# A fused attention and two-layer expert kernel: the last 768 tokens of the feed-forward in three parts of 256, with first-layer results in idle output banks

## The chip, the cores and the metric

The kernel runs on one core of one Trainium2 chip. The metric is device time in microseconds (us) for one execution, as the median of three runs. TensorE (PE in the profile), VectorE (DVE), ScalarE (ACT), GpSimd (POOL) and SyncE (SP, which issues most transfers) run side by side, each in the order of its own instructions. PE's clock has two levels, 2.4 and 1.2 GHz; the profile shows the granted one as 1.00 and 0.50.

## The reference, cut to what matters

```python
attn = softmax(mean_pool(q) @ k.T / 8) @ v            # 4 x 8 heads, 576 queries, 1152 keys
x = attn.reshape(2304, 512)                           # tokens
h = x @ w_in                                          # 512 -> 2048
x = (h * cos(h)) @ w_out                              # 2048 -> 512
e = argmax(x @ w_gate)                                # one of 8 experts per token
out = gate[:, None] * (relu(x @ w1[e]) @ w2[e])       # 512 -> 1024 -> 512, rows of one expert together
```

## The kernel before

The program has three stages: attention, feed-forward, experts. In the second and third each float32 product is three products of numbers cut into a high and a low part (high x high, high x low, low x high), so there are three matmuls where one would do.

**Feed-forward.** The 2304 tokens come in four chunks of 512 and one of 256 (`xT[d]`, 512 = `DC`, 256 = `CH`). For each chunk, `high(d)` and `low(d)` make the two parts of the tokens (`xh` by ACT, `xl` by DVE), and then sixteen steps f = 0..15 go over the 2048 hidden columns, 128 at a time. Step f is

- `layer1(d, f)` (L900): 12 matmuls of 512 (or 256) columns into one PSUM bank `h`;
- the function h cos h on ACT and DVE: a (L907, ACT), L908 to L910 (DVE), r (L911, ACT), a again (L912, ACT), L913 (DVE, the last reader of `h`: after it the bank is free), then the high part g (L914, ACT) and the low part g (L915, DVE);
- `layer2(d, f)` (L924): three matmuls for each 128 tokens into the output banks `po`, which gather over all sixteen f. It is issued two steps behind `layer1` (`LAG`, the list `todo`), three in the last chunk.

PSUM has eight banks: `ps_h` 2 (for `h`), `ps_o` 4 (one `po` for each 128 tokens), `ps_m` 2 (everything small). A chunk of 512 fills all four of `ps_o`, the last chunk two. With two banks, `layer1` of step f+2 needs L913 of step f.

When a chunk is done, `rows` copies the `po` out (L812) and one `epilogue` for each 256 tokens computes which expert each token goes to (transposes L820, products L828 to L838, counting in the class `Router`). The epilogues are generators; `go_on` takes two steps of them after each f, three in the last chunk. The epilogue of the last tokens but 256 also finds the expert of the first slot (`first`, PE line L581, then a short chain on DVE to the expert's number) and has its 4 MB of weights loaded (`load(0)`: eight transfers of 512 KB on SP, L709 and L711). From step 9 of the last chunk on, `conv(0, j)` cuts these weights into high and low part, one transfer at a time (w: ACT L718, then DVE L719).

**Experts.** Sixteen slots, in turn 256 and 128 rows of one expert. `gather`, `split` (transposes L738, then the two parts of the tokens xe: ACT L689, DVE L690), `compute` (L764 or L781 into `ph`, relu, L802 into `po`), result scattered to DRAM. Weights and tokens of slot i+1 are made ready during slot i. The xe of one slot fill all four tiles of the pool `xlp`.

The attention stage has its order from a planner. The order of the other two comes from a scheduler, from the order of the calls and the numbers of buffers.

Of the kernel before, what the change touches and what calls it, by code (L numbers as in the profile page):

```python
# [646 lines left out]
        return sel  # L647


def moe(nc, tc, magic, rp, xT, ws, w_gate, x2d, w1, w2, out, ident, W1, wp):  # L650

    FT = ws.shape[0]
    NE, D, F = w1.shape
# [7 lines left out]
    with ExitStack() as ctx:  # L661
# [7 lines left out]
        gp = pool("gate", 3)  # L669
        x2p = pool("x2", 4)  # L670
        ps_h = pool("ps_h", 2, space=PSUM)
        ps_o = pool("ps_o", 4, space=PSUM)
        ps_m = pool("ps_m", 2, space=PSUM)
        bank = lambda name: ps_m.tile([128, 512], F32, tag="h", name=name)
        otile = lambda name: op.tile([128, 512], F32, tag="o", name=name)
        wg = cq.tile([128, KC, NE], F32, name="wg")
# [5 lines left out]
            slots += big[:1] + small[:1]  # L682
            del big[:1], small[:1]
        def xtiles():
            return [[xlp.tile([128, 2, CH], F32R, tag="xl", name="xe") for _ in range(2)] for _ in range(KC // 2)]

        def split_x(x, src, cols=slice(0, CH)):
            for k, (xh, xl) in enumerate(x):
# [65 lines left out]
        def compute(i, between=()):  # L754
            n = slots[i][2]
            x, wt = X.pop(i), W.pop(i)
            hs = []
            if n == 2:
                for m in range(F2):
                    ph = ps_o.tile([128, 512], F32, tag="po", name="ph")[:, :CH]  # L760
                    c = 0
                    for k in range(KC):
                        for a, y in ((0, 0), (0, 1), (1, 0)):
                            nc.tensor.matmul(ph, lhsT=wt[k][:, a, m*128:(m+1)*128], rhs=x[k//2][y][:, k % 2], start=(c == 0), stop=(c == 3*KC-1))  # L764
                            c += 1
                    if m in (0, 2):
                        some = hp.tile([128, 2, 2, CH], F32R, tag="g", name="hh")
                    elif m == 4:
                        some = xhp.tile([128, 4, 2, CH], F32R, tag="xh", name="hh")
                    h = some[:, m % (4 if m > 3 else 2)]  # L770
                    nc.scalar.activation(h[:, 0], ph, AF.Relu)
                    nc.vector.scalar_tensor_tensor(h[:, 1], ph, 0.0, h[:, 0], op0=ALU.max, op1=ALU.subtract)
                    hs.append(h)
            else:
                for u in range(2):
                    hr = otile("hr")
                    ph = ps_o.tile([128, 512], F32, tag="po", name="ph")
                    c = 0
                    for k in range(KC):
                        for a, y in ((0, 0), (0, 1), (1, 0)):  # L780
                            nc.tensor.matmul(ph, lhsT=x[k//2][y][:, k % 2, :128], rhs=wt[k][:, a, u*512:(u+1)*512], start=(c == 0), stop=(c == 3*KC-1))  # L781
                            c += 1
                    nc.scalar.activation(hr, ph, AF.Relu)  # L783
                    p = bank("ht")
                    for k in range(4):
                        nc.tensor.transpose(p[:, k*128:(k+1)*128], hr[:, k*128:(k+1)*128], ident)
                    two = hp.tile([128, 2, 2, CH], F32R, tag="g", name="hh")
                    for k2 in range(2):
                        h = two[:, k2]
                        pv = p[:, k2*256:(k2+1)*256]  # L790
                        nc.scalar.copy(h[:, 0], pv)  # L791
                        nc.vector.tensor_sub(h[:, 1], pv, h[:, 0])
                        hs += [h[:, :, :128], h[:, :, 128:]]
            for q in range(n):
                po = ps_h.tile([128, D], F32, tag="h", name="po")
                c = 0
                for m in range(F2):
                    if q and m == 4:
                        for fn, *b in between:
                            fn(*b)  # L800
                    for a, y in ((0, 0), (0, 1), (1, 0)):
                        nc.tensor.matmul(po, lhsT=hs[m][:, y, q*128:(q+1)*128], rhs=wt[4 + m//2][:, a, (m % 2)*512:(m % 2)*512+512], start=(c == 0), stop=(c == 3*F2-1))  # L802
                        c += 1
                o = otile("ob")
                nc.scalar.activation(o, po, AF.Copy, scale=G[i][q][:, 3:4])  # L805
                nc.gpsimd.indirect_dma_start(out, bass.IndirectOffsetOnAxis(ap=index(i, q), axis=0), o, None, bounds_check=NT-1, oob_is_err=False)  # L806

        def rows(po):
            x2 = []
            for t in range(2):  # L810
                x2.append(x2p.tile([128, ROW], F32, tag="x2", name="x2"))
                nc.scalar.mul(x2[t][:, :D], po[t], -2.0)  # L812
            return x2
# [59 lines left out]
        def high(d):  # L873

            n = xT[d].shape[2]
            t = (rp if 0 < d < ND-1 else xhp).tile([128, KC, DC], F32R, tag="raw" if 0 < d < ND-1 else "xh", name="xh")[:, :, :n]
            for k in range(KC):
                nc.scalar.copy(t[:, k], xT[d][:, k])
            return t

        def low(d, xh):
            n = xT[d].shape[2]
            x = []
            for k in range(KC):
                x.append((xh[:, k], xlp.tile([128, DC], F32R, tag="xl", name="xl")[:, :n]))
                nc.vector.tensor_sub(x[k][1], xT[d][:, k], xh[:, k])
            return x

        def layer1(d, f, x):
            if d == 0 and f >= EARLY:  # L890
# [5 lines left out]
            N = xT[d].shape[2]  # L896
            h = ps_h.tile([128, DC], F32, tag="h", name="h")[:, :N]
            n = 0
            for k, a, y in [(k, a, 0) for k in range(KC) for a in range(2)] + [(k, 0, 1) for k in range(KC)]:
                nc.tensor.matmul(h, lhsT=w[:, a, k*128:(k+1)*128], rhs=x[k][y], start=(n == 0), stop=(n == 3*KC-1))  # L900
                n += 1
            if f*N % DC == 0:
                last["g"] = hp.tile([128, 2, DC], F32R, tag="g", name="g")
            o = f*N % DC
            g = last["g"][:, :, o:o+N]
# [10 lines left out]
            todo.append((d, f, g))  # L916

        def layer2(d, f, g):
            nt = g.shape[2] // 128
            if f == 0:  # L920
                pos[d] = [ps_o.tile([128, D], F32, tag="po", name="po") for t in range(nt)]
            for t in range(nt):
                for i, (y, b) in enumerate(((0, 0), (0, 1), (1, 0))):
                    nc.tensor.matmul(pos[d][t], lhsT=g[:, y, t*128:(t+1)*128], rhs=W1[f][:, b, 512:], start=(f == 0 and i == 0), stop=(f == FT-1 and i == 2))  # L924
            if f == FT-1 and d < ND-1:
                p = pos.pop(d)
                x2s = [rows(p[:2]), rows(p[2:])]
                tails.extend(epilogue(2*d + c, x2) for c, x2 in enumerate(x2s))

        x = low(0, high(0))  # L930
        for d in range(ND):
            for f in range(FT):
                layer1(d, f, x)
                if d < ND-1 and f == FT-4:
                    xh = high(d+1)
                if d < ND-1 and f == FT-1:
                    x = low(d+1, xh)
                while len(todo) > LAG + (f == LAG and d > 0 or d == ND-1):
                    layer2(*todo.pop(0))
                go_on(2 if d < ND-1 else 3)  # L940
                if d == 0 and f == 8:
                    router = Router(nc, cq, op, ps_m, NT // 128, NE)
                if d == ND-1 and f >= 9:
                    conv(0, f - 9)
        while todo:
            layer2(*todo.pop(0))
# [28 lines left out]
def body(nc, tc, q, k, v, w_in, w_out, w_gate, w1, w2, out):  # L975
    with ExitStack() as ctx:
# [13 lines left out]
        xT.append(rest.tile([128, 1024], F32, name="xT").rearrange("p (k n) -> p k n", n=NT % DC))  # L990
# [44 lines left out]
```

## Time and profile before

| | |
|---|---|
| three runs | 1242.8, 1242.84, 1246.26 us; median 1242.84 |
| the profiled execution | 1244.96 us, its span 1243.1 us |
| mean granted PE clock | 0.991 |
| busy share | PE 96%, DVE 68%, ACT 57%, POOL 35% |
| attention | 0 to 482 us |
| feed-forward, four chunks of 512 | 482 to 851 us |
| feed-forward, last chunk of 256 | 851 to 922 us |
| experts | 922 to 1243 us |

The span runs from the first to the last instruction; the execution's time is 1.86 us longer. A matmul is counted as busy until its modelled end, so that a busy PE is not PE at its peak; idle time of PE, with what ended it, is read directly.

### The profile page before, as it was taken

To read this page: it belongs to the slowest core of one execution; us is meant where nothing else is said; L and a number is where in the kernel's file an instruction comes from. 1 tells how busy PE (TensorE), PEld (TensorE's weight loads), DVE (VectorE), ACT (ScalarE), POOL (GpSimd) and SP (SyncE) were. 2 spreads that over 40 slices of the span, in tenths; PEclk is the share of its full clock that TensorE was granted. 3 is DMA by queue.
4 is the path that set the end of the run, shared out by engine and by line. 5 is a ranking of instruction groups with operands and counts; after the bars stand their busy time and mean duration, and the time that the engine had idled before them with its cause. 6 is when DMAs were issued, how large, how long until landed. Compare 5 with 4: busy or idle time off the path is not lost.

```text
span 1243.1 us, 20281 instructions
## 1 busy us (share of the span) xinstructions
PE 1199.6 (96%) x7518; PEld 901.5 (73%) x7518; DVE 845.3 (68%) x1577; ACT 712.2 (57%) x1274; POOL 431.7 (35%) x370
## 2 busy tenths in 40 slices
PE   5999999999999998999999999999798999999997
PEld 3566666666665655888788788788687888888886
DVE  4677777677776755566666666666766877777761
ACT  3466666666666566446445445445455876676751
POOL 3687887888877885000000000000003121112100
PEclk9999999999999998999999999999998999999999
DMA  6234464333442237400000000000407987778720
GB/s 253 74 97 153 165 230 153 127 126 126 144 151 101 85 109 285 184 1 18 18 1 15 22 1 9 26 1 18 170 18 279 387 292 252 267 271 281 263 87 6
DMA packets 70932, 163.59 MB, mean 132 GB/s; under 512 B 7670, under 2 KB 24814, under 8 KB 68785
## 3 DMA queue, kind: packets, MB, share of 16 engines
q1 hardware_dynamic: 66832, 150.92, 34.8%
q0 software_dynamic: 4000, 11.38, 2.4%
q8 instruction: 59, 0.97, 0.3%
q14 instruction: 41, 0.33, 0.1%
HBM read 135.65 MB, written 28.39 MB: 132 GB/s over the span
## 4 chain that ended last, share of the span: by engine, by line
PE 89%; issue 3%; ACT 3%; DMA 2%; DVE 2%; POOL 1%; SPq 0%; POOLq 0%; ACTq 0%; DVEq 0%
PE h L900 16%; PE po L924 15%; PE o L341 12%; PE s L322 12%; PE po L802 9%; PE ph L764 7%; PE pmx L264 5%; PE s L324 3%; PE psum L351 3%; PE ph L781 2%; PE pmx L267 1%; DMA raw<-in_moe_w_dram 1%; ACT w L718 1%; DVE MX L275 1%; PE pt L820 1%
## 5 line engine op out<-in xcount | busy, mean ns | idle before, releaser
L335 POOL TENSOR_TENSOR es<-es,E 128x576 f32<-128x576 f32 x192 | 274.6, 1430 | 35.0 <-ACT E L328 25.0
L328 ACT ACTIVATE E<-s 128x576 f32<-128x576 f32 x288 | 183.2, 652 | 123.4 <-PE s L324 112.9
L275 DVE TENSOR_REDUCE MX<-pmx 128x2 f32<-128x768 f32 x192 | 183.1, 957 | 68.5 <-PE pmx L264 68.5
L924 PE MATMUL po<-wf,g 128*128 128x512 f32 x864 | 211.1, 392 | 0.0
L322 PE MATMUL s<-Q,K 64*128 64x288 f32 x1152 | 192.2, 418 | 1.3 <-ACT E L328 1.3
L924 PEld LDWEIGHTS po<-wf,g 128*128 128x128 f32 x864 | 161.8, 189 | 32.9 <-DVE g L915 0.2
L719 DVE TENSOR_TENSOR w<-raw,w 128x1024 fp32r<-128x1024 f32 x128 | 155.7, 1221 | 42.0 <-ACT w L718 40.3
L730 POOL DMA_INDIRECT xg<-x2d,idx x25 | 29.4, 1175 | 444.2 <-DVE tri L594 354.3
L341 PE MATMUL o<-E,vt 128*64 128x288 f32 x1152 | 169.2, 417 | 0.4 <-ACT ob L345 0.3
L900 PE MATMUL h<-xh,wf 128*128 128x512 f32 (+1 forms) x640 | 154.5, 380 | 12.5 <-DVE a L913 12.5
L718 ACT CAST w<-raw 128x1024 fp32r<-128x1024 f32 x128 | 133.1, 1053 | 28.8 <-PE po L802 15.3
L324 PE MATMUL s<-MR,ON 64*128 64x288 f32 x576 | 148.5, 511 | 0.0
L802 PE MATMUL po<-w,hh 128*128 128x512 f32 x600 | 142.9, 392 | 0.0
L900 PEld LDWEIGHTS h<-xh,wf 128*128 128x128 f32 x640 | 112.2, 192 | 36.3 <-DVE a L913 14.9
L802 PEld LDWEIGHTS po<-w,hh 128*128 128x128 f32 x600 | 111.0, 188 | 22.5 <-ACT hh L791 0.3
L764 PE MATMUL ph<-xe,w 128*128 128x256 f32 x864 | 116.8, 289 | 8.0 <-ACT hr L783 3.9
L764 PEld LDWEIGHTS ph<-xe,w 128*128 128x128 f32 x864 | 110.5, 195 | 12.0 <-ACT hr L783 5.2
L322 PEld LDWEIGHTS s<-Q,K 64*128 64x128 f32 x1152 | 97.9, 188 | 25.1 <-issue 13.6
L341 PEld LDWEIGHTS o<-E,vt 128*64 128x64 f32 x1152 | 72.0, 136 | 60.3 <-issue 24.8
L911 ACT ACTIVATE r<-r 128x512 f32<-128x512 f32 (+1 forms) x80 | 43.2, 540 | 122.8 <-DVE r L910 111.1
L806 POOL DMA_INDIRECT out_dram<-ob,idx x25 | 27.2, 1088 | 206.4 <-ACT ob L805 190.8
L264 PE MATMUL pmx<-KH,QH 64*128 64x384 f32 x384 | 83.5, 433 | 11.1 <-ACT QH L251 7.6
(196 smaller groups left out, 1553.5 us busy)
## 6 DMA issues: line engine op xcount, KB each, us to landing
raw<-in_moe_w_dram SPq DMA_DIRECT2D x128, 512.0 KB
wf<-ws SPq DMA_DIRECT2D x16, 1024.0 KB
vt<-in_v_dram SPq DMA_DIRECT2D x16, 576.0 KB
qr<-in_q_dram SPq DMA_DIRECT2D x15, 576.0 KB
K<-in_k_dram SPq DMA_DIRECT2D x15, 576.0 KB
cv_t<-in_moe_w_in_dram SPq DMA_DIRECT2D x16, 512.0 KB
ws<-cv_o SPq DMA_DIRECT2D x32, 256.0 KB
cv_t<-in_moe_w_out_dram SPq DMA_DIRECT2D x16, 512.0 KB
```

The source lines that it names most:

```text
L264: nc.tensor.matmul(p[:, h, :KG], lhsT=QH[R[h], t*128:(t+1)*128], rhs=KH[R[h], g*KG:(g+1)*KG], start=True, stop=True)
L275: nc.vector.reduce_max(out.rearrange("p (w g) -> p w g", g=3)[:, 2*t:2*t+2, g], p[:, :, :KG], axis=AX.X)
L322: nc.tensor.matmul(p[:, h, :NQ], lhsT=T["k", i][R[h], j*128:(j+1)*128], rhs=T["q", i][R[h], qs], start=True, stop=False)
L324: nc.tensor.matmul(p[:, h, :NQ], lhsT=ON[R[h]], rhs=MR[i % 3][R[h], qs], start=False, stop=True)
L328: nc.scalar.activation(e, T.pop(("s", i, hq, j))[:, :, :NQ], AF.Exp, scale=1.0/16)
L335: nc.gpsimd.tensor_add(T["es", i, hq], T["e", i, hq, 0] if j == 1 else T["es", i, hq], T["e", i, hq, j])
L341: nc.tensor.matmul(T["o", i, hq][64*h:64*h+64], lhsT=T["v", i][:, h, j], rhs=T["e", i, hq, j][:, h], start=(j == 0), stop=(j == J-1))
L719: nc.vector.tensor_sub(w[:, 1], t, w[:, 0])
L764: nc.tensor.matmul(ph, lhsT=wt[k][:, a, m*128:(m+1)*128], rhs=x[k//2][y][:, k % 2], start=(c == 0), stop=(c == 3*KC-1))
L802: nc.tensor.matmul(po, lhsT=hs[m][:, y, q*128:(q+1)*128], rhs=wt[4 + m//2][:, a, (m % 2)*512:(m % 2)*512+512], start=(c == 0), stop=(c == ...
L900: nc.tensor.matmul(h, lhsT=w[:, a, k*128:(k+1)*128], rhs=x[k][y], start=(n == 0), stop=(n == 3*KC-1))
L924: nc.tensor.matmul(pos[d][t], lhsT=g[:, y, t*128:(t+1)*128], rhs=W1[f][:, b, 512:], start=(f == 0 and i == 0), stop=(f == FT-1 and i == 2))
```

## The change: what it does

1. The list `chunks` cuts the feed-forward into six pieces: three of 512, then tokens 1536 to 1791, 1792 to 2047 (both from `xT[3]`, whose parts are made once), and 2048 to 2303. The pieces of 256 take `layer2` three steps behind. In the last two pieces `go_on` takes one step of an epilogue after each f, elsewhere two.
2. `ps_o` becomes two pools of two banks. A piece of 256 puts its `po` in one pair, the next piece in the other (`side`). The idle pair holds `h` of the odd steps f > 5 in a piece of 256, and of step 1 of the very first piece. In the experts `ph` alternates between `ps_h` and the second pair, `po` is in the first.
3. The low parts of the experts' tokens move to the tile of the last 256 tokens' `xT` (pool `rest`, one buffer), so the high parts of two slots fit in `xlp`.

```diff
-        ps_o = pool("ps_o", 4, space=PSUM)
+        ps_o = [pool(n, 2, space=PSUM) for n in ("ps_o", "ps_p")]
+        hbank = lambda n: (ps_h, ps_o[1])[n % 2].tile([128, 512], F32, tag="h" if n % 2 == 0 else "po", name="h")
+        obank = lambda n: ps_o[n].tile([128, D], F32, tag="po", name="po")
...
-            return [[xlp.tile([128, 2, CH], F32R, tag="xl", name="xe") for _ in range(2)] for _ in range(KC // 2)]
+            low = rest.tile([128, KC, CH], F32R, tag="xT", name="xel")
+            return [(xlp.tile([128, 2, CH], F32R, tag="xl", name="xe"), low[:, 2*k:2*k+2]) for k in range(KC // 2)]
...
+        chunks = [(d, 0, DC) for d in range(NT//DC - 1)] + [(NT//DC - 1, 0, CH), (NT//DC - 1, CH, CH), (NT//DC, 0, CH)]
...
-            h = ps_h.tile([128, DC], F32, tag="h", name="h")[:, :N]
+            other = f % 2 and (f == 1 if c == 0 else N == CH and f > LAG + 3)
+            h = (ps_o[1 - side(c)].tile([128, DC], F32, tag="po", name="h") if other else ps_h.tile([128, DC], F32, tag="h", name="h"))[:, :N]
...
+        def side(c):
+            return (ND-1 - c) % 2 if chunks[c][2] == CH else 0
...
-                while len(todo) > LAG + (f == LAG and d > 0 or d == ND-1):
+                while len(todo) > LAG + (f == LAG and c > 0 or N == CH):
                     layer2(*todo.pop(0))
-                go_on(2 if d < ND-1 else 3)
+                go_on(1 if c > ND-3 else 2)
```

**Place 1, PE, the start of the feed-forward.** The rows are the first matmuls of `layer1` for f = 0, 1, 2, 3 (`wf_93` to `wf_96` are the weights of these steps) and of `layer2` for f = 0. Before:

```order
L351 MATMUL psum_5225<-E_5219,ones64_127 64x288 x2
L900 MATMUL h_5332<-xh_5319,wf_93 128x512 x8
...
L900 MATMUL h_5357<-xh_5319,wf_94 128x512 x8
...
L900 MATMUL h_5382<-xh_5319,wf_95 128x512 x8
...
L924 MATMUL po_5407<-wf_93,g_5345 128x512 x3
...
L900 MATMUL h_5423<-xh_5319,wf_96 128x512 x8
```

In the change:

```order
L909 MATMUL h_5360<-xh_5322,wf_94 128x512
L341 MATMUL o_5127<-E_5219,vt_4408 64x288 x2
...
L909 MATMUL h_5335<-xh_5322,wf_93 128x512 x8
...
L909 MATMUL h_5360<-xh_5322,wf_94 128x512 x7
...
L909 MATMUL h_5385<-xh_5322,wf_95 128x512 x8
...
L909 MATMUL h_5426<-xh_5322,wf_96 128x512 x4
L937 MATMUL po_5410<-wf_93,g_5348 128x512 x2
```

One matmul of step 1 moves ahead of the last of attention, and the first four of step 3 ahead of `layer2` of step 0. Behind that first matmul the order of steps 0, 1, 2 stands as it was.

**Place 2, PE and ACT, the last piece of 256.** On PE `pn0` is the matmul (L581) that begins the choice of the first expert. Before it stands behind `layer1` of f = 7 (`h_8619`):

```order
L900 MATMUL h_8619<-xl_8207,wf_5577 128x256
L924 MATMUL po_8379<-wf_5460,g_8428 128x512 x2
L924 MATMUL po_8380<-wf_5460,g_8428 128x512 x2
L554 LDWEIGHTS scr_8509
L554 MATMUL ptt_8533<-scr_8509 72x256
L581 LDWEIGHTS oneb_5674
L581 MATMUL pn0_8539<-cum_5694,oneb_5674 128x8
```

In the change behind f = 6 (`h_8975`):

```order
L909 MATMUL h_8975<-xl_8672,wf_5541 128x256
L937 MATMUL po_8814<-wf_96,g_8754 128x512
L554 LDWEIGHTS scr_8866
L554 MATMUL ptt_8920<-scr_8866 72x256
L581 LDWEIGHTS oneb_5677
L581 MATMUL pn0_8926<-cum_5697,oneb_5677 128x8
```

On ACT the first four casts of the expert's weights (`w`) stand before as follows; `a_8632` is step 7, `a_8663` step 8, `a_8693` step 9:

```order
L912 ACTIVATE a_8632<-r_8633 128x256
L914 CAST g_8601<-a_8602 128x256
L718 CAST w_8710<-raw_8568 128x1024
L914 CAST g_8601<-a_8632 128x256
L907 ACTIVATE a_8663<-h_8649,magic_66 128x256
L718 CAST w_8744<-raw_8568 128x1024
L907 ACTIVATE a_8693<-h_8680,magic_66 128x256
L718 CAST w_8777<-raw_8571 128x1024
L718 CAST w_8811<-raw_8571 128x1024
L911 ACTIVATE r_8664<-r_8664 128x256
L912 ACTIVATE a_8663<-r_8664 128x256
```

In the change `a_9019` is step 7, `a_9050` step 8, `a_9080` step 9:

```order
L916 ACTIVATE a_9050<-h_9036,magic_66 128x256
L921 ACTIVATE a_9019<-r_9020 128x256
L721 CAST w_9097<-raw_8955 128x1024
L923 CAST g_8988<-a_9019 128x256
L721 CAST w_9131<-raw_8955 128x1024
L920 ACTIVATE r_9051<-r_9051 128x256
L916 ACTIVATE a_9080<-h_9067,magic_66 128x256
L921 ACTIVATE a_9050<-r_9051 128x256
L721 CAST w_9164<-raw_8958 128x1024
L721 CAST w_9198<-raw_8958 128x1024
L923 CAST g_9049<-a_9050 128x256
```

The third and fourth cast stood ahead of r and a of step 8; now they stand behind these two and ahead of its cast g.

**Place 3, ACT, a slot of 128 rows in the experts.** hr is the relu of such a slot (two of them), xe the high part of the next slot's tokens (two casts for each half). Before:

```order
L783 ACTIVATE hr<-ph 128x512
L718 CAST w<-raw 128x1024
L689 CAST xe<-xt 128x2x128 x2
L718 CAST w<-raw 128x1024
L783 ACTIVATE hr<-ph 128x512
L689 CAST xe<-xt 128x2x128 x2
```

In the change:

```order
L692 CAST xe<-xt 128x2x128 x2
L750 ACTIVATE ex,g<-xg,g 128x8
L786 ACTIVATE hr<-h 128x512
L721 CAST w<-raw 128x1024 x3
L692 CAST xe<-xt 128x2x128 x2
L786 ACTIVATE hr<-h 128x512
```

The first two casts of xe move ahead of the first hr. On DVE the subtraction that makes the low part keeps its place behind the same w (one w, two low parts, one w, two low parts).

## Rows read from the trace of the kernel before

**Rows 1.** Windows by stage: busy us and instructions per engine, PE clock, DMA share, GB/s.
```profile
482.00:499.00 17.00, 12.98 (x47) 10.23 (x46) 9.78 (x18) 9.43 (x16) 3.33 (x8) 0.80 1.01 425
499.00:851.00 352.00, 352.00 (x1671) 285.55 (x1670) 228.55 (x476) 167.01 (x280) 1.13 (x3) 1.00 0.06 24
851.00:884.00 33.00, 32.95 (x226) 27.84 (x225) 22.65 (x91) 15.16 (x36) 0.00 (x0) 1.00 0.09 33
884.00:922.00 38.00, 29.53 (x164) 25.28 (x164) 27.17 (x65) 23.74 (x50) 2.25 (x2) 0.91 0.35 125
```

**Rows 2.** Waits of PE, whole run: us in total, times, longest.
```profile
PE h L900 <- DVE a L913: 12.5, 4, 5.0
```

**Rows 3.** Chain that ended last, 480 to 506: start us, us, what.
```profile
481.73 5.68 PE h L900 x24
...
490.67 0.70 DVE a L913
...
491.41 5.36 PE h L900 x12
...
499.51 2.72 PE h L900 x12
```

**Rows 4.** Windows at the start of the feed-forward, columns as in Rows 1.
```profile
488.00:490.00 2.00, 0.00 (x0) 0.00 (x0) 1.93 (x4) 1.97 (x3) 0.00 (x0) 0.92 1.02 430
490.00:496.00 6.00, 4.59 (x11) 3.63 (x12) 2.77 (x5) 2.82 (x6) 0.00 (x0) 0.50 1.01 426
```

**Rows 5.** Chain that ended last, 851 to 884.
```profile
851.22 1.43 PE h L900 x12
...
868.37 1.37 PE po L924 x6
```

**Rows 6.** Timeline of PE, 881 to 898: start, us, idle before it and releaser.
```profile
881.51 0.17 PE L581 MATMUL pn<-cum,oneb 128*128 128x8 bf16 x1
...
886.50 1.21 PE L900 MATMUL h<-xh,wf 128*128 128x256 f32 x8 [2.52 <-DVE a L913]
...
897.37 2.08 PE L900 MATMUL h<-xh,wf 128*128 128x256 f32 x8 [5.00 <-DVE a L913]
```

**Rows 7.** Timeline of ACT, 883 to 899.
```profile
887.96 1.05 ACT L718 CAST w<-raw 128x1024 fp32r<-128x1024 f32 x1 [0.81 <-DMA raw<-in_moe_w_dram]
...
892.38 1.04 ACT L718 CAST w<-raw 128x1024 fp32r<-128x1024 f32 x1 [1.38 <-DMA raw<-in_moe_w_dram]
895.13 1.04 ACT L718 CAST w<-raw 128x1024 fp32r<-128x1024 f32 x1 [1.71 <-DMA raw<-in_moe_w_dram]
896.08 0.37 ACT L911 ACTIVATE r<-r 128x256 f32<-128x256 f32 x1
```

**Rows 8.** Chain that ended last, 883 to 925.
```profile
897.37 2.93 PE h L900 x12
900.30 2.53 PE po L924 x6
```

**Rows 9.** Groups by shape, 600 to 850: busy us, mean ns, idle before.
```profile
L910 DVE SCALAR_TENSOR_TENSOR r<-a,r 128x512 f32<-128x512 f32 x43 | 29.9, 694 | 1.2
```

**Rows 10.** Groups by shape, 851 to 922.
```profile
L910 DVE SCALAR_TENSOR_TENSOR r<-a,r 128x256 f32<-128x256 f32 x16 | 6.8, 424 | 0.1
L914 ACT CAST g<-a 128x256 fp32r<-128x256 f32 x16 | 6.4, 403 | 4.5 <-DVE a L913 4.5
```

**Rows 11.** Windows of the last chunk, columns as in Rows 1.
```profile
882.00:888.00 6.00, 3.47 (x26) 2.83 (x24) 4.91 (x21) 1.84 (x6) 2.25 (x2) 1.00 0.42 144
...
892.00:896.00 4.00, 0.38 (x2) 0.00 (x0) 2.70 (x6) 1.91 (x2) 0.00 (x0) 0.98 1.03 391
908.00:920.00 12.00, 12.00 (x72) 10.37 (x71) 7.94 (x22) 6.92 (x19) 0.00 (x0) 1.00 0.00 0
```

**Rows 12.** Waits of PE in the experts, 955 to 1243, and one in the timeline.
```profile
PE ph L764 <- ACT hr L783: 3.9, 6, 0.7
...
1024.57 1.93 PE L764 MATMUL ph<-xe,w 128*128 128x256 f32 x14 [0.72 <-ACT hr L783]
```

More of the change, by code (lines that the diff above doesn't have):

```diff
@@ L647, in finish, with moe @@
         return sel
-def moe(nc, tc, magic, rp, xT, ws, w_gate, x2d, w1, w2, out, ident, W1, wp):
+def moe(nc, tc, magic, rp, xT, ws, w_gate, x2d, w1, w2, out, ident, W1, wp, rest):
     FT = ws.shape[0]
@@ L759, in compute @@
                 for m in range(F2):
-                    ph = ps_o.tile([128, 512], F32, tag="po", name="ph")[:, :CH]
+                    ph = hbank(m)[:, :CH]
                     c = 0
@@ L776, in compute @@
                     hr = otile("hr")
-                    ph = ps_o.tile([128, 512], F32, tag="po", name="ph")
+                    ph = hbank(u)
                     c = 0
@@ L794, in compute @@
             for q in range(n):
-                po = ps_h.tile([128, D], F32, tag="h", name="po")
+                po = obank(0)
                 c = 0
@@ L865, in moe @@
         tails, todo, pos = [], [], {}
+        chunks = [(d, 0, DC) for d in range(NT//DC - 1)] + [(NT//DC - 1, 0, CH), (NT//DC - 1, CH, CH), (NT//DC, 0, CH)]
+        starts = [sum(n for _, _, n in chunks[:i]) for i in range(len(chunks))]
+        ND = len(chunks)
         def go_on(n):
@@ L875, in high @@
             n = xT[d].shape[2]
-            t = (rp if 0 < d < ND-1 else xhp).tile([128, KC, DC], F32R, tag="raw" if 0 < d < ND-1 else "xh", name="xh")[:, :, :n]
+            old = 0 < d < len(xT)-1
+            t = (rp if old else xhp).tile([128, KC, DC], F32R, tag="raw" if old else "xh", name="xh")[:, :, :n]
             for k in range(KC):
@@ L887, in low, with layer1 @@
             return x
-        def layer1(d, f, x):
-            if d == 0 and f >= EARLY:
+        def layer1(c, f, x):
+            d, o, N = chunks[c]
+            if c == 0 and f >= EARLY:
                 W1.append(wp[f].tile([128, 2, 1024], F32R, tag="w", name="wf"))
@@ L895, in layer1 @@
             w = W1[f]
-            N = xT[d].shape[2]
-            h = ps_h.tile([128, DC], F32, tag="h", name="h")[:, :N]
+            other = f % 2 and (f == 1 if c == 0 else N == CH and f > LAG + 3)
+            h = (ps_o[1 - side(c)].tile([128, DC], F32, tag="po", name="h") if other else ps_h.tile([128, DC], F32, tag="h", name="h"))[:, :N]
             n = 0
             for k, a, y in [(k, a, 0) for k in range(KC) for a in range(2)] + [(k, 0, 1) for k in range(KC)]:
-                nc.tensor.matmul(h, lhsT=w[:, a, k*128:(k+1)*128], rhs=x[k][y], start=(n == 0), stop=(n == 3*KC-1))
+                nc.tensor.matmul(h, lhsT=w[:, a, k*128:(k+1)*128], rhs=x[k][y][:, o:o+N], start=(n == 0), stop=(n == 3*KC-1))
                 n += 1
-            if f*N % DC == 0:
+            at = f*N % DC
+            if at == 0:
                 last["g"] = hp.tile([128, 2, DC], F32R, tag="g", name="g")
-            o = f*N % DC
-            g = last["g"][:, :, o:o+N]
+            g = last["g"][:, :, at:at+N]
             a, r = otile("a")[:, :N], bank("r")[:, :N]
@@ L915, in layer1, with layer2 @@
             last["dve"] = nc.vector.tensor_sub(g[:, 1], a, g[:, 0]).ins
-            todo.append((d, f, g))
-        def layer2(d, f, g):
+            todo.append((c, f, g))
+        def side(c):
+            return (ND-1 - c) % 2 if chunks[c][2] == CH else 0
+        def layer2(c, f, g):
             nt = g.shape[2] // 128
             if f == 0:
-                pos[d] = [ps_o.tile([128, D], F32, tag="po", name="po") for t in range(nt)]
+                pos[c] = [obank((side(c) + t//2) % 2) for t in range(nt)]
@@ L922, in layer2 @@
             for t in range(nt):
                 for i, (y, b) in enumerate(((0, 0), (0, 1), (1, 0))):
[L924 to L928, printed above, removed]
+                    nc.tensor.matmul(pos[c][t], lhsT=g[:, y, t*128:(t+1)*128], rhs=W1[f][:, b, 512:], start=(f == 0 and i == 0), stop=(f == FT-1 and i == 2))
@@ L930, in moe @@
+            if f == FT-1 and c < ND-1:
+                p = pos.pop(c)
+                x2s = [rows(p[t:t+2]) for t in range(0, nt, 2)]
+                tails.extend(epilogue(starts[c]//CH + t, x2) for t, x2 in enumerate(x2s))
         x = low(0, high(0))
-        for d in range(ND):
+        for c, (d, o, N) in enumerate(chunks):
+            new = c < ND-1 and chunks[c+1][1] == 0
             for f in range(FT):
[L933 to L937, printed above, removed]
-                while len(todo) > LAG + (f == LAG and d > 0 or d == ND-1):
+                layer1(c, f, x)
+                if new and f == FT-4:
+                    xh = high(chunks[c+1][0])
+                if new and f == FT-1:
+                    x = low(chunks[c+1][0], xh)
+                while len(todo) > LAG + (f == LAG and c > 0 or N == CH):
@@ L939, in moe @@
                     layer2(*todo.pop(0))
-                go_on(2 if d < ND-1 else 3)
-                if d == 0 and f == 8:
+                go_on(1 if c > ND-3 else 2)
+                if c == 0 and f == 8:
                     router = Router(nc, cq, op, ps_m, NT // 128, NE)
-                if d == ND-1 and f >= 9:
+                if c == ND-1 and f >= 9:
                     conv(0, f - 9)
@@ L989, in body @@
         xT = [rp.tile([128, 2048], F32, tag="raw", name="xT").rearrange("p (k n) -> p k n", n=DC) for c in range(NT // DC)]
-        xT.append(rest.tile([128, 1024], F32, name="xT").rearrange("p (k n) -> p k n", n=NT % DC))
+        xT.append(rest.tile([128, 1024], F32, tag="xT", name="xT").rearrange("p (k n) -> p k n", n=NT % DC))
         wp = [ctx.enter_context(tc.tile_pool(name=f"w{j}", bufs=1)) for j in range(EARLY)]
@@ L994, in body @@
         attention(nc, tc, q, k, v, xT, ident, w_in, w_out, ws, x2d, W1)
-        moe(nc, tc, magic, rp, xT, ws, w_gate, x2d, w1, w2, out, ident, W1, wp)
+        moe(nc, tc, magic, rp, xT, ws, w_gate, x2d, w1, w2, out, ident, W1, wp, rest)
 _INS = ["q", "k", "v", "moe_w_in", "moe_w_out", "moe2_w_gate", "moe2_w1", "moe2_w2"]
```

## The prediction

> **What bounds the kernel now.** I read the windows by stage first. From 499 to 851 us PE is busy for all 352 us at clock 1.00, and from 851 to 884 for 32.95 of 33 [rows 1]: there the order of work is full, and only fewer or cheaper matmuls would save time. The feed-forward loses time in two stretches: 482 to 499 (PE 12.98 of 17 us, mean clock 0.80) and 884 to 922 (29.53 of 38, clock 0.91). Then the waits of PE: `layer1` waited four times for L913, the last reader of `h`, 12.5 us in all [rows 2]. One such wait lies in the first stretch, three in the second. All are waits for a free bank, since that is what L913 gives back.
>
> *Start.* Steps 0 and 1 run back to back until 487.41, and step 2 starts at 491.41, when L913 of step 0 has ended [rows 3]: 4.00 us idle. In that gap the clock falls, and from 490 to 496 it is 0.50 [rows 4]: step 2 takes 5.36 us, where the next one takes 2.72 [rows 3], another 2.64. The stretch loses 6.64 us.
>
> *End.* PE waits 2.52 and 5.00 us for L913 [rows 6], and the sum of all, 12.5 less the 4.0 of the start, gives 8.5 with one short wait more. After the long one PE runs at half speed: a `layer1` takes 2.93 us and a `layer2` 2.53 [rows 8], where they take 1.43 and 1.37 [rows 5], another 2.66. So this stretch loses 11.1 us. Its cause is ACT, which casts the first expert's weights between the steps: it sits idle for the weights 0.81, 1.38 and 1.71 us before three casts, and r of step 8 comes only at 896.08, behind the fourth [rows 7], so that L913 and the bank are late.
>
> **The change part by part.**
>
> *A third bank at the start: −4.3 us.* Step 1 now has a bank of the output pair, so step 2 finds a free one and can run from about 487.1, right behind step 1 (one matmul of which now runs ahead). Step 3 has the bank of step 0, free at 491.4 as before; four of its matmuls stand ahead of `layer2` of step 0. PE's new sequence by the old durations: step 2 ends at 489.9, PE idles 1.5 until 491.4, does four matmuls of 0.227 us (2.72 / 12) and waits about 1.0, until 493.3, in `layer2` of step 0 for g, which ACT and DVE give a little later than before because they now also take step 2 in between. Then `layer2` of step 0 (2.72), the other eight matmuls of step 3 (1.82) and `layer2` of step 1 (2.72) end at 500.6. Before, step 3 starts at 499.51 [rows 3], and 5.44 us later, at 504.95, the same point is reached. The gain is 4.3. That supposes the clock stays high: the idle time of 2.52 us that ended at 886.50 [rows 6] left it at 1.00 [rows 11], and mine are 1.5 and 1.0. If it falls all the same, step 3 and `layer2` double and cost about 3: gain 1.2. If no g is late, 5.3. Bounds 1.2 to 5.3.
>
> *The split of 512 tokens: +2.2 us.* Layer 1 goes from 16 steps of 2.72 us to 32 of 1.43 [rows 3, 5]: 45.76 − 43.52 = 2.24 us more of PE, on the path, since PE is full there. Layer 2 keeps its matmuls. By the Trainium skill, TensorE: Matmul & The Clock Gate, section Back-to-back issue gap, an isolated matmul takes N/2.4 + 2.5 ns, so that halving N would add only 2.5 ns for each of 192 pairs, 0.5 us; the rows show 119 ns against 227, which is more, and I use the rows. The sum by the page would be 1.7 us lower.
>
> *Banks and epilogues in the two new parts: +0.5 us.* Up to step 6 a part has two banks as the last chunk had, and there, with two epilogues at three steps each, PE was busy 32.95 of 33 us and DVE 22.65 [rows 1]. The new parts have two epilogues at two steps and one at one step. I take 0.5 us for short waits at the joints; bounds 0 and 3.
>
> *The last part: −7.1 us.* The choice of the expert now begins behind step 6, one step earlier. Before, from that matmul (881.51) the weights' casts start at 887.96, 892.38 and 895.13 for the first, third and fourth transfer [rows 6, 7], 6.4, 10.9 and 13.6 us later; the last two waited for the data, so that is when they land. The chain between (small DVE steps, SP's load of the number, the transfers) is unchanged. Call the matmul 0. PE at 2.80 us a step (1.43 + 1.37) ends step 8 at 6.0 and wants `layer2` of step 8 at 14.4. ACT gets to the first cast at about 7, when its data is there, and now does r and a of step 8 ahead of the third, so banks are free: odd steps have a pair of their own. What still waits is g of step 8, behind the fourth cast: 13.6 + 1.04 + 0.40, and DVE's low part 0.42 [rows 7, 10], 15.5. PE waits 1.1 us there. Behind it ACT has four more casts of 1.04 between the steps and DVE as many subtractions; followed step by step in the new order, PE waits about 1.4 us for g of step 9 and 1.5 in short waits after it. That makes 4.0 us, none of it over 2.5, so the clock stays high. The gain is 11.1 − 4.0 = 7.1. Bounds: 10.1 (only the first wait), and 2, if a wait grows past that of 5.00 us and takes the clock along.
>
> *Experts: 0.* Before each slot of 128 rows but one PE waits 0.72 us [rows 12], in name for hr, in fact for the low part of xe, which DVE makes behind the subtraction of a weight. The high part moves ahead, but the low tile still has one buffer and its place on DVE behind the same weight, so the low part is no earlier. Bounds: −3.4 (nearly all of the 3.9 us goes) and +1.0 (hr of the second half now stands behind three casts of w).
>
> Sum: −4.3 + 2.2 + 0.5 − 7.1 = −8.7 us. The profiled execution took 1244.96, of which the span is 1243.1; it would become 1236.3. It lies 2.1 us over the median of the three runs; against the median 1242.84 − 8.7 = 1234.1, and I say 1234.5, rounded. A difference of 0.3%, 3.7 us, is about what a measurement of this kernel tells from none.
>
> **The rivals.**
>
> *ACT's queue keeps the end as it is (1239).* The casts of the third and fourth transfer still hold everything behind them, g above all, and DVE takes 1.2 us more for each. If one wait then passes 3 us and the clock falls, the gain at the end is 2 to 3: 1242.8 − 4.3 + 2.7 − 2.5 = 1238.7. For it: PE's idle time here is set by the data's landing (from 892 to 896 the DMA share is 1.03 [rows 11]), which the change doesn't move against the choice. Against it: r and a of step 8 now precede the casts.
>
> *The start gains little (1237).* The first result takes as long as before; only the wait moves to step 3 and `layer2`. If the clock falls in these two waits, 1.2 instead of 4.3: 1237.2. For it: 2.5 us of idle time in 4 us. Against: neither part is longer than the 2.52 that left the clock high.
>
> *DVE becomes the bound (1253, slower).* A step on 512 columns takes 0.694 us, on 256 0.424 [rows 9, 10]; four such steps make 16 x 4 x (0.848 − 0.694) = 9.9 us more DVE work for the 512 tokens, and the fifth, shorter one about as much again as a quarter of it, 12.4 in all. It would be on the path if DVE were full: then the end gains nothing either, since the weights' subtractions come on top, and the time is 1242.8 − 4.3 + 2.2 + 12.4 = 1253.1. The point from which it decides: DVE's work for a step above PE's 2.80 us. Against it: from 908 to 920 DVE is busy 7.94 of 12 us with PE full [rows 11], and 22.65 of 33 with two epilogues [rows 1]. The Trainium skill, VectorE: DVE Perf Modes, section on the TRN2 errata, says that each instruction pays a fixed extra and advises tiles of at least 512 elements; by that rule alone the split is a loss. The trace agrees on the fixed part.
>
> *The experts' waits go too (1231).* If the earlier high part lets DVE go on sooner, 3.4 more: 1231.
>
> **How the numbers follow.** My forecast 0.52, the experts' waits as well 0.10, the small start 0.14, the end kept 0.15, DVE the bound 0.09. Faster by over 0.3% (below 1239.1) are the first three and a small half of the fourth less what they leave over that line: 0.79; the same 0.13; slower 0.08. The range takes in 1231 and 1239 with the bounds at the end (10.1 instead of 7.1) on the low side and a part wait of 2 more on the high side: 1229 to 1241. DVE as the bound is left out.
>
> **What the new profile would show.** Start: no idle row over 2 us before `layer1`, clock 1.00 from 482 to 500. New parts: `layer1` groups of 1.43 us, PE busy in all but 1 us of 100. Last part: the weights' first cast without a long DMA wait, PE waits of about 1 us in `layer2` for g, none of 5 us, clock 1.00. Experts: the same 0.72 us rows. Wrong it would be if waits for L913 come up within the new parts, if the clock is 0.50 anywhere in the feed-forward, or if the stretch between the last part and the second slot, which hangs on the last epilogue and its loads, grows by what the feed-forward loses.

## The result and the profile after

The change runs in 1232.64 us, median of four (1232.47 to 1235.71); the kernel before in 1243.68 (1242.80 to 1246.26). The ratio is 0.9914, with an interval of 0.9891 to 0.9936: 11.0 us faster. The prediction said 1234.5, range 1229 to 1241.

The profiled execution is the slowest of the four (1235.71 us, span 1233.5). To see where the time went, I cut each span at three points of PE: the end of attention's last matmul (L351), the end of `layer2` of step 1 in the first piece (read as the start of the `layer1` behind it), and the end of the last `layer2`.

| stretch (us) | before | after | difference | predicted |
|---|---|---|---|---|
| up to the end of attention | 481.73 | 483.91 | +2.18 | 0 |
| start of the feed-forward | 23.05 | 17.75 | −5.30 | −4.3 |
| rest of the feed-forward | 416.60 | 409.63 | −6.97 | +2.2 +0.5 −7.1 = −4.4 |
| experts | 321.72 | 322.21 | +0.49 | 0 |

Of the start's 5.30, 0.23 is the one matmul of step 1 that now stands ahead of attention's last ones and is counted there. The other 1.95 us of the first row are this execution's: the clock fell in attention (last section), and in run 5, the same program, they are absent. The windows of the change, columns as in [rows 1]:

```profile
482.00:499.00 17.00, 15.69 (x73) 11.88 (x73) 12.77 (x22) 11.32 (x20) 5.42 (x17) 1.00 0.97 395
490.00:496.00 6.00, 4.69 (x22) 3.53 (x21) 5.07 (x10) 4.63 (x8) 0.00 (x0) 1.00 1.01 426
499.00:751.00 252.00, 252.00 (x1191) 204.67 (x1190) 162.50 (x334) 120.89 (x205) 1.13 (x3) 1.00 0.08 33
751.00:855.00 104.00, 103.95 (x699) 91.50 (x698) 75.29 (x240) 56.55 (x142) 0.00 (x0) 1.00 0.04 16
855.00:884.00 29.00, 29.00 (x197) 26.27 (x196) 21.54 (x82) 15.17 (x38) 2.20 (x2) 1.00 0.13 46
884.00:912.00 28.00, 26.66 (x155) 22.25 (x153) 23.77 (x55) 21.62 (x47) 0.18 (x1) 1.00 0.39 143
400.00:410.00 10.00, 9.14 (x52) 5.06 (x51) 4.97 (x8) 6.01 (x13) 5.91 (x6) 0.66 0.28 111
```

In both stretches that lost time before ([rows 1], first and fourth row) PE is now nearly full, and the clock is 1.00 throughout the feed-forward. The waits of PE from 480 to 925 us (in all, times, longest), against the one row of [rows 2]:

```profile
PE h L909 <- DVE a L922: 1.5, 2, 1.3
PE h L767 <- ACT xe L692: 0.9, 1, 0.9
PE po L937 <- ACT g L923: 0.5, 1, 0.5
```

12.5 us of bank waits have become 1.5. The start in the chain that ended last, against [rows 3]:

```profile
483.90 5.46 PE h L909 x23
...
493.37 1.20 PE h L909 x4
494.57 2.72 PE po L937 x12
...
499.10 2.72 PE po L937 x12
```

Step 2 follows step 1 without a gap. The first four matmuls of step 3 wait 1.3 us for the bank of step 0, and `layer2` of step 0 starts right behind them, at 2.72 us: g is there and the clock is high. At the end of the feed-forward, ACT and then PE (timeline, columns as in [rows 6]):

```profile
886.86 0.37 ACT L920 ACTIVATE r<-r 128x256 f32<-128x256 f32 x1
...
887.51 0.37 ACT L921 ACTIVATE a<-r 128x256 f32<-128x256 f32 x1
888.58 1.05 ACT L721 CAST w<-raw 128x1024 fp32r<-128x1024 f32 x1 [0.70 <-DMA raw<-in_moe_w_dram]
890.31 1.05 ACT L721 CAST w<-raw 128x1024 fp32r<-128x1024 f32 x1 [0.68 <-DMA raw<-in_moe_w_dram]
891.27 0.40 ACT L923 CAST g<-a 128x256 fp32r<-128x256 f32 x1
```

```profile
891.72 1.65 PE L937 MATMUL po<-wf,g 128*128 128x512 f32 x6
...
895.33 1.86 PE L937 MATMUL po<-wf,g 128*128 128x512 f32 x6 [0.54 <-ACT g L923]
```

r and a of step 8 now run ahead of the third and fourth cast. These still wait for their data, but behind them stands only g of step 8, which ends at 891.67, just as PE comes for it.

The split made `layer2` longer too. Steps in the new parts (chain that ended last):

```profile
796.13 1.43 PE h L909 x12
797.56 1.39 PE po L937 x6
798.95 1.43 PE h L909 x12
```

A step of 256 columns takes 2.82 us from start to start; a step of 512 takes 5.44 (before: 499.51 [rows 3] to 504.95). So two small steps take 0.20 us more than one large one, and sixteen pairs 3.2 us.

### The profile page after: what moved, and what is told of

The parts are those of the page before. It is cut to its first block, busy times and chain, and to the rows that moved or that the text cites. A ratio compares the mean times of both kernels' runs of the same rounds, so it can differ in the third digit from the quotient of the medians.

```text
span 1233.5 us, 20791 instructions
## 1 busy us (share of the span) xinstructions
PE 1199.3 (97%) x7710; PEld 907.6 (74%) x7710; DVE 849.8 (69%) x1657; ACT 721.3 (58%) x1338; POOL 430.7 (35%) x370
## 4 chain that ended last, share of the span: by engine, by line
PE 87%; DVE 3%; issue 3%; ACT 3%; DMA 2%; POOL 1%; SPq 0%; POOLq 0%; DVEq 0%
PE h L909 15%; PE po L937 15%; PE o L341 12%; PE s L322 12%; PE po L805 9%; PE h L767 6%; PE pmx L264 5%; PE s L324 3%; PE psum L351 3%; PE h L784 2%; DMA raw<-in_moe_w_dram 2%; PE pmx L267 1%; DVE w L722 1%; ACT w L721 1%; DVE MX L275 1%
## 5 line engine op out<-in xcount | busy, mean ns | idle before, releaser
L937 PE MATMUL po<-wf,g 128*128 128x512 f32 x864 | 214.3, 392 | 0.7 <-ACT g L923 0.5
L322 PE MATMUL s<-Q,K 64*128 64x288 f32 x1152 | 192.7, 418 | 1.3 <-ACT E L328 1.3
L937 PEld LDWEIGHTS po<-wf,g 128*128 128x128 f32 x864 | 158.6, 188 | 32.6 <-ACT g L923 1.5
L909 PE MATMUL h<-xh,wf 128*128 128x512 f32 (+1 forms) x768 | 155.7, 341 | 1.5 <-DVE a L922 1.5
L909 PEld LDWEIGHTS h<-xh,wf 128*128 128x128 f32 x768 | 122.0, 189 | 21.3 <-issue 2.9
L322 PEld LDWEIGHTS s<-Q,K 64*128 64x128 f32 x1152 | 98.0, 188 | 25.2 <-issue 13.7
L767 PE MATMUL h<-xe,w 128*128 128x256 f32 x576 | 109.1, 286 | 3.9 <-ACT xe L692 3.0
L920 ACT ACTIVATE r<-r 128x512 f32<-128x512 f32 (+1 forms) x96 | 45.8, 477 | 113.6 <-DVE r L919 105.3
L767 PEld LDWEIGHTS h<-xe,w 128*128 128x128 f32 x576 | 92.1, 193 | 6.7 <-ACT xe L692 3.9
```

Source lines behind the costliest of these rows:

```text
L322: nc.tensor.matmul(p[:, h, :NQ], lhsT=T["k", i][R[h], j*128:(j+1)*128], rhs=T["q", i][R[h], qs], start=True, stop=False)
L937: nc.tensor.matmul(pos[c][t], lhsT=g[:, y, t*128:(t+1)*128], rhs=W1[f][:, b, 512:], start=(f == 0 and i == 0), stop=(f == FT-1 and i == 2))
```

## The experiments

All are the change or the kernel before with a few lines edited. "Rest" is the third row of the table above, so it holds what the split costs PE (3.2 us) where there is one; "start" the second. In runs 3, 4 and 11 two to four matmuls of the experts, at most 0.6 us, stand ahead of the last `layer2` and are in the rest. The ratio is to the kernel before on the same chip.

| run | median us | ratio, interval | start | rest |
|---|---|---|---|---|
| kernel before | 1243.7 to 1244.7 | 1 | 23.05 | 416.60 |
| 5, the change again | 1233.28 | 0.9914 (0.9901 to 0.9926) | 17.79 | 409.71 |
| 1, no third bank at the start | 1238.65 | 0.9950 (0.9937 to 0.9964) | 23.03 | 409.71 |
| 6, third bank at the start alone | 1239.41 | 0.9965 (0.9954 to 0.9977) | 17.79 | 416.62 |
| 12, split alone | 1244.27 | 1.0003 (0.9993 to 1.0012) | 22.33 | 414.73 |
| 2, no idle pair at the end | 1237.60 | 0.9950 (0.9937 to 0.9964) | 17.76 | 414.35 |
| 3, no split | 1231.39 | 0.9902 (0.9887 to 0.9917) | 17.77 | 409.05 |
| 4, before, casts behind r | 1243.62 | 0.9994 (0.9984 to 1.0003) | 22.32 | 417.77 |
| 7, before, casts behind a | 1240.11 | 0.9967 (0.9956 to 0.9978) | 22.32 | 414.29 |
| 8, run 2 with casts behind a | 1235.37 | 0.9931 (0.9920 to 0.9943) | 17.76 | 412.34 |
| 9, old room of the low parts | 1233.09 | 0.9924 (0.9908 to 0.9941) | 17.77 | 409.40 |
| 10, two epilogue steps at a time | 1236.07 | 0.9936 (0.9922 to 0.9949) | 17.76 | 412.57 |
| 11, run 3 with casts behind g | 1227.70 | 0.9873 (0.9859 to 0.9888) | 17.78 | 408.11 |

My theory: two separate shortages of banks, at the start and at the end, and at the end ACT's queue with the casts as the cause. The rivals: the clock by itself, the earlier choice of the expert by itself, and two banks being too few whatever ACT does.

**The start (runs 1, 5, 6).** Run 1:

```diff
-other = f % 2 and (f == 1 if c == 0 else N == CH and f > LAG + 3)
+other = f % 2 and c > 0 and N == CH and f > LAG + 3
```

> The change without the third bank at the start: h of step 1 of the first piece is in the h pool again, all else stays. Theory (the bank alone makes the start's gain, and half of that is the clock that no longer falls): PE waits 4.0 us before step 2 again, the clock is 0.50 for some 6 us, and the time goes from 1232.6 up by 5.1 us to 1237.7. Rival (the clock at the start is chance, the bank gives only the idle time less the 1.3 us that now stand before step 3): 2.7 us more, 1235.3.

The wait is back, and so is the slow step behind it (timeline of PE):

```profile
491.15 3.78 PE L909 MATMUL h<-xh,wf 128*128 128x512 f32 x8 [4.02 <-DVE a L922]
```

The start takes 23.03 us again, the rest is the same to 0.1 us. Run 5 is the unchanged change.

> The change itself once more, on the chip of the three runs beside it, so that they can be set against it. Both theories: 0.989 to 0.993 of the kernel before; no wait of 4 us before step 2, clock 1.00 through the feed-forward.

It came as expected, and in this execution attention ends at 481.45, so the 1.95 us were that one execution's. Run 6 has `chunks` and `go_on` of before and only the third bank:

```diff
+other = f == 1 and c == 0
```

> The kernel before with only the third bank at the start (and the low parts' room): no split, no idle pair for h in the last piece. Theory (the parts add up): the start's 5 to 6 us are gained, the waits of 2.5 and 5 us at the end and the low clock behind the second stay, 6 us under the kernel before, ratio 0.995. Rival (a stretch gained at the start is lost again at the end, since both feed the same transfers): ratio 0.998 or more.

The theory holds for the start; the median gains 4.8 us where 6 were expected. In its profile the rest is that of before to 0.02 us, but by two parts that differ and cancel out: the long wait is 3.53 us and not 5.00, and the clock falls a second time.

**What makes the end (runs 12, 2, 4, 7, 8).** Run 12 sets `other = False`.

> The change with no step's h in an output bank at all: only the split, its slower pace and the low parts' room are left. Theory (the split costs 2 us of PE and gets some of that back, since its choice of the expert makes no wait of 2.5 us; start and end keep their bank waits): 4.0 us before step 2 and 3.8 us before step 10, 1237.6 + 5.5 = 1243, within 1.5 us of the kernel before. Rival (the split by itself makes half of the gain): 1239.

The split with its slower pace is worth nothing in the median. Its rest is 1.9 us shorter, though PE has 3.2 us more to do: the wait of 2.52 us is gone, the long one is 3.88.

```profile
894.80 2.08 PE L909 MATMUL h<-xh,wf 128*128 128x256 f32 x8 [3.88 <-DVE a L922]
```

Run 2 leaves the start's bank in (`other = f == 1 and c == 0`).

> The change without the idle pair for h in the pieces of 256: all steps there use the two banks of the h pool; split, start and the room of the low parts stay. Theory (the end gains because r and a of step 8 no longer stand behind the third and fourth cast of the expert's weights, and that order hangs on the free banks): the fourth cast starts 13 us behind the choice of the expert, step 10 wants the bank of step 8 at 8.5 us and gets it at about 15, one wait of 6 us, the clock falls behind it; most of the 9 us at the end are lost, 1240 to 1242. Rival (the choice comes a step earlier, and that makes the gain; the banks matter little): 1233 to 1235.

Between the two: 1237.6. The rest is 2.25 us shorter than before, in spite of the split's 3.2, so about half of what the end gains (5.5 of 10.2 us) comes without the idle pair. The waits in its timeline:

```profile
889.43 1.75 PE L909 MATMUL h<-xh,wf 128*128 128x256 f32 x8 [3.79 <-DVE a L922]
...
897.86 1.21 PE L909 MATMUL h<-xh,wf 128*128 128x256 f32 x8 [1.00 <-DVE a L922]
```

The long one is there, but no wait of 2.52 us ahead of it, with no more banks than before. So that first wait had a cause of its own. DVE of the kernel before shows it, at step 6, whose bank PE wants at 883.98 (the first row is ACT's, which makes a of that step):

```profile
878.99 0.47 ACT L907 ACTIVATE a<-h,magic 128x256 f32<-128x256 f32 x1
...
882.06 0.28 DVE L908 TENSOR_SCALAR a<-a 128x256 f32<-128x256 f32 x1
...
882.61 0.69 DVE L558 TENSOR_TENSOR acc<-acc,ptt 72x512 bf16<-72x512 bf16 x1 [0.20 <-PE ptt L554]
...
884.23 0.42 DVE L909 SCALAR_TENSOR_TENSOR r<-a,h 128x256 f32<-128x256 f32 x1
...
886.02 0.42 DVE L913 SCALAR_TENSOR_TENSOR a<-a,h 128x256 f32<-128x256 f32 x1
```

DVE starts L908 2.6 us after a is there (879.46), and L909 another 2.17 us later. Nearly all it does in between is the epilogue's counting (L534 to L545) and the choice of the expert (L558, L583 on). This is read from the trace: no run moves that work by itself. Runs 4 and 7 test the casts themselves, in the kernel before. `issue_after(x)` makes the scheduler place what is in it behind instruction x of its engine; run 4:

```diff
-                    conv(0, f - 9)
+                    with tc.issue_after(last["act"]):
+                        conv(0, f - 9)
...
-        conv(0, 7)
+        with tc.issue_after(last["act"]):
+            conv(0, 7)
```

> The kernel before, with one edit: each of the eight casts of the first expert's weights stands on ACT behind r of the step at which it is called (steps 9 to 15, the last two at 15), so that no r, a or g of steps 8 and 9 waits behind a cast whose data has not landed. Banks and chunks are as before. Theory (ACT's queue with the early casts is the cause of the 8.5 us of waits and of the low clock behind them): waits for L913 in the last chunk go, the start's 4.0 us stay, 1242.8 - 11 = 1232, if the first slot's weights are ready as early as the last tokens are. Rival (too few banks are the cause, whatever ACT's order): 1241 or more.

The theory missed: nothing is gained. PE's timeline:

```profile
888.58 1.22 PE L900 MATMUL h<-xh,wf 128*128 128x256 f32 x8 [2.52 <-DVE a L913]
...
900.99 1.21 PE L900 MATMUL h<-xh,wf 128*128 128x256 f32 x8 [0.76 <-DVE a L913]
905.27 1.21 PE L900 MATMUL h<-xh,wf 128*128 128x256 f32 x8 [1.21 <-DVE a L913]
```

and ACT's:

```profile
902.31 0.37 ACT L911 ACTIVATE r<-r 128x256 f32<-128x256 f32 x1 [0.93 <-DVE r L910]
902.59 1.04 ACT L718 CAST w<-raw 128x1024 fp32r<-128x1024 f32 x1
903.53 0.39 ACT L912 ACTIVATE a<-r 128x256 f32<-128x256 f32 x1
```

The 2.52 us end at 888.58, and the first cast starts at 894.03: the casts can't be their cause. The 5.00 us are gone, but my edit put each cast between r and a of its own step, into the chain that gives the bank back, and the steps from 901 on take 4.28 us each. Run 7 moves the casts out of that chain:

```diff
-            nc.scalar.activation(a, r, AF.Square)
+            acts[d, f] = nc.scalar.activation(a, r, AF.Square).ins
...
-                    conv(0, f - 9)
+                    with tc.issue_after(acts[d, max(f - 3, 7)]):
+                        conv(0, f - 9)
```

(and the eighth behind `acts[ND-1, 13]`).

> The kernel before with one edit that keeps the casts out of the steps' chains: the third cast of the first expert's weights stands on ACT behind a (the second) of step 8, the fourth behind that of step 9, and so on, the eighth behind that of step 13; the first two stay. Two banks as before. Theory (r and a of step 8 behind casts that wait for data make the wait of 5.0 us and, by it, the low clock; the wait of 2.5 us before it has another cause, DVE's work for the choice): the 2.5 us stay, the 5.0 us shrink to under 1, the clock stays high, 6 to 7.5 us under the kernel before, ratio 0.9945. Rival (two banks are too few whatever the order): waits of together over 6 us stay, ratio over 0.998.

Half right: 4.1 us faster, not 6 to 7.5. The 5.00 us became 2.00, 0.54, 0.44 and 0.77; 0.7 us of the gain are the start, where the clock happened to be low for a shorter time. What is left of the long wait is DVE's: r of step 8 waits behind the second subtraction.

```profile
889.62 1.22 DVE L719 TENSOR_TENSOR w<-raw,w 128x1024 fp32r<-128x1024 f32 x1
...
891.29 0.42 DVE L910 SCALAR_TENSOR_TENSOR r<-a,r 128x256 f32<-128x256 f32 x1
```

Run 8 has the edit of run 7 in run 2.

> The change without the idle pair in the pieces of 256 (as in the run without end banks, 1237.6 us), with the casts in the order of the run beside this one: third cast behind a of step 8, fourth behind a of step 9 and so on. Theory (ACT's order makes the end's gain, and the banks give it only by letting that order come about): the wait of 3.8 us goes, about 4 us less, 1233 to 1234, as fast as the change. Rival (the banks themselves are needed): 1236 or more, with waits for L922 that move to later steps.

Neither theory is enough. Of the 4.6 us by which the rests of run 2 and run 5 differ, 2.0 come with this order of the casts; the other 2.6 come only with the banks (no other order was run without them). Three waits for a bank stay, and 0.77 us for g:

```profile
887.84 1.22 PE L909 MATMUL h<-xh,wf 128*128 128x256 f32 x8 [1.57 <-DVE a L922]
894.42 1.22 PE L909 MATMUL h<-xh,wf 128*128 128x256 f32 x8 [0.68 <-DVE a L922]
...
900.85 1.22 PE L909 MATMUL h<-xh,wf 128*128 128x256 f32 x8 [0.44 <-DVE a L922]
```

**The split and the pace (runs 3, 10, 11).** Run 3 undoes the split and keeps all banks:

```diff
+chunks = [(d, 0, DC) for d in range(NT//DC)] + [(NT//DC, 0, CH)]
...
+                go_on(3 if c == ND-1 else 2)
```

> The change without the split: four pieces of 512 and one of 256 as before, two epilogues in the last piece at three steps a time, but with the third bank at the start, the idle pair for odd steps from 7 on in the last piece, and the low parts' room. Theory (banks, not the split, make the end's gain, and the split costs 2.2 us): waits of about 0.8 and 1.0 us in layer2 of steps 8 and 9, no wait over 2 us, layer1 of the fourth piece of 512 at 2.72 us; 1230 to 1232, a little under the change's 1232.6. Rival (the split, with one epilogue instead of two and the earlier choice, makes the end's gain): waits of 2.5 and 5 us stay, 1238 to 1240.

The theory holds. The choice puts as much work on DVE as before, but no wait for a bank is left in the last piece; what waits is g, in `layer2` of steps 8 and 9:

```profile
888.33 1.66 PE L937 MATMUL po<-wf,g 128*128 128x512 f32 x6 [1.42 <-ACT g L923]
...
892.17 1.66 PE L937 MATMUL po<-wf,g 128*128 128x512 f32 x6 [0.64 <-ACT g L923]
```

Its median is 1.9 us under the change's, with intervals that overlap. Run 10 has `go_on(2)` throughout.

> The change with two steps of an epilogue after each f in the last two pieces too, instead of one. The expert is chosen some three steps earlier and its casts stand at steps 5 to 10, partly where odd steps still have no pair of their own. Theory (what counts is that no r or a stands behind a cast that waits for data, and that DVE's work for the choice does not come in one burst): waits of 2 to 4 us in the last piece, 1234 to 1237. Rival (the earlier the choice, the better, since the data is then there): 1231 to 1232.5.

As the theory said: a wait of 2.42 us, the clock 0.79 to 0.87 around it, 2.8 us more. Run 11 is run 3 with the casts behind g (`acts` holds L923, otherwise as in run 7).

> The run without the split (1231.4 us), and in it the third cast of the first expert's weights behind g of step 8, the fourth behind that of step 9, and so on to the eighth behind that of step 13. Theory (its waits of 1.4 and 0.6 us in layer2 of steps 8 and 9 are g behind a cast that waits for data): both go, 1229.4 to 1230. Rival (the casts are then late by themselves and the first slot waits for its weights): 1231 or more.

Both waits are gone; two of 0.53 and 0.77 us come at steps 14 and 15. At 1227.70 us it is the fastest, and its interval lies clear of the change's. Why the median lies 3.7 us under run 3's, I can't say in full: the two profiled executions (1230.22 and 1228.34) differ by 1.9, of which 0.9 are in the rest, 0.55 in the experts and 0.4 in attention. Run 3's profiled execution is the fastest of its four.

**The room of the low parts (run 9).** `xtiles` is that of before.

> The change with the experts' low parts back in xlp beside the high parts, as before; all else of the change stays. Theory (the new room is worth nothing: DVE makes the low part behind the same subtraction either way): within 1 us of the change's 1233.3, and the waits of 0.7 us before the slots of 128 rows stay. Rival (the room lets the high parts be early and saves something): 1234.5 or more.

No difference. The waits of PE in the experts of the change, and of run 9:

```profile
PE h L767 <- DVE xel L693: 4.4, 6, 1.0
```

```profile
PE h L766 <- ACT hr L785: 3.9, 6, 0.7
```

The wait of 1.0 is that of `split(1)`, before the second slot. The others are the same stall under another name (five of 0.68 us against five of 0.72): with the new room hr is no longer last, the low part is.

## Why the prediction was right, and where it was not

- **What bounds the kernel.** The two stretches were right. "Its cause is ACT" was right for the second wait alone, and there in part: the 2.52 us end before the first cast starts (run 4) and by the trace are DVE's work for the counting and the choice; with ACT's order mended two banks still cost 2.6 us (run 8).
- **Third bank, −4.3.** Mechanism right, size 0.8 us short: 5.07 in the trace (the 5.30 less the moved matmul), 5.4 between the medians of runs 1 and 5, and 4.5 by their ratios. The step that failed is the 1.0 us for g in `layer2` of step 0, which did not come.
- **The clock.** It stayed high behind the 1.3 us, in all nine profiles with this bank. But the ground I gave, a wait of 2.52 us that left it at 1.00, does not carry: in run 6 the same wait is followed by half speed (below).
- **The split, +2.2.** 1.0 us short. A `layer1` of 256 columns takes 1.43 us in the new parts as in [rows 5], which makes the 2.2. The step that failed is "Layer 2 keeps its matmuls": the same six matmuls take 1.39 us there, and half of the 2.72 is 1.36, so the split costs 3.2. Why they take longer, no run shows. Run 3 against the change gives 1.9 in the median, where longer waits for g (2.06 us against 0.54) offset a part. By the Trainium skill, TensorE: Matmul & The Clock Gate, section Back-to-back issue gap, whose formula is for the gap of isolated matmuls, an estimate would be 0.5; the trace does not agree, with 119 and 227 ns for each matmul of `layer1`.
- **Joints, +0.5.** 0.05 us in 104.
- **The last part, −7.1.** The term that was mis-sized most: −6.97 − 3.2 − 0.05 makes −10.2, at my bound of 10.1. The mechanism held, the waits were too long. I had 4.0 us of them; from 884 to 912 PE idles 1.34, about 0.5 of it behind the last `layer2`, and 11.1 less the 0.85 that are left is again 10.2. I had made PE wait 1.1 us for the low part of g of step 8, which only the third matmul of a `layer2` reads: PE starts at 891.72 behind the high part, without a wait. For g of step 9 I had 1.4 and it was 0.54; of the 1.5 in short waits 0.17 came.
- **Experts, 0.** +0.5 here, +1.9 in run 5 (323.65 us), nothing for the new room (run 9). The wait of `split(1)` stayed, 1.77 and 0.99 us. In the eight profiles with the split the experts take 322.1 to 323.7 us, in the six without it 319.6 to 321.7, so the split may cost up to some 2 us here too; the cause stays open. The new banks of `ph` and `po` in the experts were undone in no run.
- **The rivals.** *The end kept* is what runs 2 and 12 show without the banks. *DVE the bound* fell: 75.29 of 104 us in the new parts. *The start gains little* would have needed the low clock. *The experts' waits go too* fell: five of 0.68 us are left.

In this trace the gain is 5.1 at the start and 7.0 in the rest, less 0.5 in the experts: 11.6 us but for the clock's fall in attention, where the medians give 11.0. The terms were off by −0.8, +1.0, −0.4, −3.1 and +0.5, together −2.9: that it is no more is luck in part, since errors of both signs meet in the sum. With its slower pace the split pays for itself and no more (run 12); the banks are what gains.

## What to carry to other kernels

A wait for a buffer names the instruction that gave it back, not what made that late: look at what stands ahead of it in the queues of all engines on its chain, and test each by moving it. Where a queue holds work that waits for a transfer, put it behind what others wait for; even then the engine next in line (here DVE with the subtractions) may hold the same chain. Idle buffers cover such delays whatever their cause, and here more cheaply than smaller pieces do.

## What the hardware showed that I had not expected

The same wait can cost the clock or not. In run 6's last piece PE waits 2.52 us, as it does in the kernel before and in runs 4 and 7, where the next eight matmuls take 1.21 or 1.22 us [rows 6], in the kernel before at clock 1.00 [rows 11]. In run 6 they take 2.08, and the mean clock of the stretch is 0.73:

```profile
879.77 2.08 PE L909 MATMUL h<-xh,wf 128*128 128x256 f32 x8 [2.52 <-DVE a L922]
```

```profile
880.00:885.00 5.00, 5.00 (x29) 4.83 (x30) 3.33 (x6) 3.68 (x7) 0.89 (x1) 0.73 0.99 329
```

In attention the profiles of the change and of the kernel before both have waits of 1.33, 0.27 and 0.59 us between 398 and 403. In the change's the clock from 400 to 410 is 0.66 (last row of its windows), in that of the kernel before 1.00. Below are its window, and the matmuls behind the third wait, first in the kernel before and then in the change:

```profile
400.00:410.00 10.00, 8.99 (x70) 5.48 (x70) 6.90 (x10) 7.95 (x17) 6.66 (x7) 1.00 0.36 136
```

```profile
402.78 0.71 PE L351 MATMUL psum<-es,ones 128*64 128x288 f32 x4 [0.59 <-DVE cv_o L407]
```

```profile
402.09 1.23 PE L351 MATMUL psum<-es,ones 128*64 128x288 f32 x4 [0.59 <-DVE cv_o L407]
```

From there to the same matmul further on (L322, at 407.66 before and at 409.75 in the change) it is 4.88 us before and 7.66 in the change. This fall is behind the 1.95 us in attention, and so behind most of the 3 us by which the profiled execution lies above the other three.

Behind the 4.02 us at the start the clock is low for a while in all five profiles that have this wait, but not for the same time: the slow step takes from 4.6 (runs 4, 7, 12) to 5.36 us (before). The Trainium skill, TensorE: Matmul & The Clock Gate, section Part 1: The HAM clock gate, says that the point at which the clock rises differs from run to run; the trace agrees with these numbers.
